# A fused decode step and its gradients: the first batch's w1 sums spread over more iterations, and a later start of the second pass

## The chip, the cores and the metric

The kernel runs on one core of one Trainium2 chip. The metric is the device time of one execution in microseconds. Beside the times there is one profiled execution, in which every instruction and every DMA packet was recorded; all readings of engines and queues below come from it.

## What is computed

The program is one decoder block for a single new token in each of two sequences (batches), forward and backward in one launch. Cut to what matters:

```python
x  = A_x                                     # 2 x 1 x 640, bf16
q  = layernorm(x) @ wq                       # 32 heads of 128
s  = q . K^T * 128**-0.5                     # K, V: 2 x 32 heads x 4096 keys x 128
p  = softmax(s)
h  = x + (p . V) @ wo                        # attention and residual
h2 = h + relu(layernorm(h) @ w1) @ w2        # MLP, 640 -> 1728 -> 640
out_0 = h2
# and the gradients of h2, seeded with grad_out, by x, K, V, wq, wo, w1, w2:
# gV[key, :] = p[key] * go          gK[key, :] = gs[key] * q
```

The caches and their gradients are by far the largest data: for each of the 64 pairs of batch and head a K tile and a V tile of 1 MB (4096 x 128 in bf16) are read, and a gK tile and a gV tile of the same size are written. Here go is the gradient that reaches a head's output, and gs = p * (dp - dot), with dp = V . go and dot the sum of p * dp.

## The kernel before, in words

**Two passes over the pairs.** The gradient go of a batch is known only when the attention of all its heads, the output projection, the MLP and their backward have been gone through. So the kernel works in two passes. The first pass (p1_iter, iterations i = 0 to 65) takes one pair an iteration in a software pipeline of three stages: in iteration i the scores of pair i are computed (K is transposed on PE in groups, line 423, copied out of PSUM, line 428, and multiplied with the query, line 436), the softmax numerators of pair i-1 are formed (the row maximum, line 559, is spread over the partitions by a matmul, line 503, and its minimum taken, line 505; the exponential, line 512, gives ep; two multiplies on VectorE, line 464, weight the K tile with it and give the pk tiles), and the products of pair i-2 are summed on PE (line 457 with V, line 486 with K). The second pass (p2_iter, steps j = 0 to 64) takes one pair a step: it transposes the V tile again, computes dp, and writes gV and gK as outer products on VectorE (line 809), some of whose gV columns ScalarE makes (line 870) in the steps that run alone, up to j = 32. The gK and gV tiles leave by the POOL queue (lines 850 and 871).

**The middle between them.** For each batch a generator, middle_gen, computes what lies between: the last attention outputs, the second layernorm, the MLP's hidden layer, its backward and the go of each head. It is background work: the main loop calls bg_step after each of the eight parts k = 0 to 7 of an iteration, and it advances as far as a credit allows. Its costly parts are sums on VectorE (ttr, line 644: a multiply of two tiles with a sum along the row): 15 of 128 x 576 with w1 for the gradient of the layernorm's output, and after them 32 of 128 x 640 with wo, one a head, in groups; after a group, a few small instructions mark its heads as done ("go"). Before each such sum the generator asks turn() for a slot; the main loop sets the number of slots, slot[0], anew in each part of an iteration, and slots not used are gone.

**Where the passes meet.** Batch 0's middle is queued at the end of iteration 33. Then come M0_ITERS iterations of the first pass alone, in which it runs. At iteration P2_AT = H + 2 + M0_ITERS = 41 the second pass begins: from there a step j runs beside every two iterations i, and after iteration 65 the remaining steps run alone. If the go of a step's head is not yet done when the step begins, bg_until forces the middle on. P2_AT also switches some helpers: before it the pk column that sums ep (line 474) and the copy of p (line 547) are made on POOL, from it on ScalarE (line 476) and VectorE.

**Buffers and queues.** K and V tiles come through the SP queue, in a list made beforehand, each into the next free of 12 buffers of 1 MB; a load waits, at the head of its queue, for the buffer's last reader. The V tiles of the last six heads of batch 0 (KEPT) stay in their buffers from the first pass to the second, which takes these six heads first; the other V tiles are loaded a second time (W tiles). At P2_AT and after, some buffers pass to the gK and gV tiles. The w1 matrix is loaded once, near iteration 35. A further set of generators, for the gradients of w1, w2, wo, wq and x, starts when batch 1's w1 sums are done, and stores by the ACT queue.

Of the kernel before, what the change touches and what calls it, by code (L numbers as in the profile page):

```python
# [15 lines left out]
def kernel(  # L16
# [582 lines left out]
    def a_heads(i):  # L599

        if a_next[0] < o_next[0]:
            a_group()
        elif o_next[0] < NP1 // OG and i >= o_next[0] * OG + OG + 2:
            b, g = divmod(o_next[0], H // OG)
            if b > 0 or i >= W_AT[g * OG * 4 // H] + 4:
                o_group()
# [40 lines left out]
    slot = [99]  # L647
# [399 lines left out]
    done = set()  # L1047
# [16 lines left out]
    def bg_step(k, rate):  # L1064
        step[0] += int(k == 1)
        q = (bg, bg2, bg3)[k]
        credit[k] = min(credit[k] + rate, 1.0 if k else 2.0) if q else 0.0
        while q and credit[k] > 0.0:
            took = bg_one(q)
            credit[k] -= took  # L1070
            if took == 0.0:
                break
# [5 lines left out]
            assert bg and bg_one(bg) >= 0.0, mark  # L1078
        forced[0] = False

    M0_ITERS = 7
    P2_AT = H + 2 + M0_ITERS
    RATES = (0.2, 0.8, 0.2, 0.8, 0.45)
    RATE2 = 0.65
# [28 lines left out]
    def pump():  # L1113
        while queue:
            what, k = queue[0]
            if what == "w":
                load_weights(k)
            else:
                tag = "ld"
                if free["ld"] < 1:  # L1120
                    return
                if what == "w2":
                    w2_tiles[k] = load_w2(k, tag)
                else:
                    load_tile(what, k, tag)
            queue.pop(0)
# [12 lines left out]
    def p2_step():  # L1139
        nonlocal g2  # L1140
        try:
            next(g2)
        except StopIteration:
            g2 = None

    for n, (i, j) in enumerate(plan):
# [42 lines left out]
        if i is None:  # L1189
            spread[0] = 2  # L1190
            at_k[0] = 1
            k = 0
# [10 lines left out]
        for k, _ in enumerate(p1_iter(i, i < H + 1, 0)):  # L1203
            for _ in range(at.get(k, 0)):
                if g2 is not None:
                    p2_step()
            if k == 5:
                a_heads(i)
            pump()

            spread[0] = 1 if i < P2_AT else 2
            at_k[0] = k
            if i >= P2_AT:
                slot[0] = int(k == 6 or (k == 1 and j is None))
            elif i > H + 1:
                slot[0] = {1: 2, 3: 1, 4: 1, 6: 1}.get(k, 0)
            else:
                slot[0] = int(k in (1, 6))
            bg_step(0, rate)
            bg_step(1, 0.0)  # L1220
# [43 lines left out]
```

## Time and profile before

| | |
|---|---|
| median of 3 runs | 896.87 us (896.23 to 898.17) |
| profiled execution, its own time | 895.05 us |
| its span, first to last instruction or transfer | 893.3 us |
| mean granted TensorE clock | 0.776 of full |
| PE, DVE, ACT, POOL busy | 83%, 77%, 54%, 23% of the span |
| moved by DMA | 362.89 MB, mean 406 GB/s |
| iterations 34 to 40, first pass alone with batch 0's middle | 211.67 to 256.96 us, by the row maxima |
| first gV store | 267.95 us |

How to read it: the page's slices cut the span into 40 equal parts; a digit is the busy share of an engine in tenths, and the GB/s row gives what the DMA queues moved. The windows view gives the same for stretches that one chooses. The timeline lists instructions with their start, their length and, in brackets, the time their engine stood idle before them and what ended that wait; starts of one instruction that comes once an iteration give the iteration's length. The busy share of PE is not a measure of how near it is to its limit, since the ends of its pipelined matmuls are modelled. The waits view sums, for each pair of instructions, how long one waited for the other. An iteration's row maximum is the instruction at line 559; the one of iteration 30, for example, started at 190.11 us.

### The profile page before, as it was taken

Reading aid. Unit: us, or ns where it says so; the run is one execution under the profiler, and the core shown is the slowest. Engines: PE = TensorE matmul, PEld = TensorE weight load, DVE = VectorE, ACT = ScalarE, POOL = GpSimd, SP = SyncE. Lnnn points to the kernel's source line nnn. Section 1 sums busy time; section 2 is a strip of 40 time slices with the busy share of each in tenths; the row PEclk is TensorE's granted clock in tenths of the full one; section 3 lists DMA queues with packets and bytes.
Section 4 is the critical chain, followed back from the end, with each engine's and each line's share of the span. In section 5 each row is a group of like instructions: output and inputs, shape, how many; then the busy total and the mean of one; then the engine's idle time right before and its main releaser. Section 6 shows DMA issues by size and latency. Waiting matters only on the chain.

```text
span 893.3 us, 24580 instructions
## 1 busy us (share of the span) xinstructions
PE 742.4 (83%) x10145; PEld 619.6 (69%) x10145; DVE 686.8 (77%) x1284; ACT 482.9 (54%) x1242; POOL 208.0 (23%) x349
## 2 busy tenths in 40 slices
PE   4999899999998997988968777877887889578780
PEld 4888788788887886877757766666765566366460
DVE  2566788777878897786878887878896469999872
ACT  1344334344555554554536767777675666367560
POOL 1344434443211111010011242222221111111120
PEclk9999999999999999998995556555565565565565
DMA  9999999999889999999999999999999999999996
GB/s 378 425 419 417 416 408 417 426 423 367 314 322 357 424 424 425 424 423 425 420 406 394 420 422 416 411 415 421 416 424 415 408 386 425 425 425 424 427 422 294
DMA packets 56432, 362.89 MB, mean 406 GB/s; under 512 B 5696, under 2 KB 11776, under 8 KB 15488
## 3 DMA queue, kind: packets, MB, share of 16 engines
q1 hardware_dynamic: 34664, 212.17, 58.2%
q0 software_dynamic: 18432, 134.23, 36.1%
q10 hardware_dynamic: 3224, 14.92, 4.1%
q8 instruction: 80, 1.31, 0.5%
q14 instruction: 32, 0.26, 0.1%
HBM read 212.16 MB, written 149.13 MB: 404 GB/s over the span
## 4 chain that ended last, share of the span: by engine, by line
PE 45%; DMA 26%; DVE 12%; ACT 9%; issue 4%; SPq 0%; POOL 0%; ACTq 0%; POOLq 0%; DVEq 0%
PE t_ps L423 19%; DMA Vt<-in_A_v_cache_dram 11%; PE m_ps L457 10%; DMA out_dram<-gV 7%; DMA out_dram<-gK 5%; PE s_ps L436 3%; ACT gV L870 3%; DVE gV L809 3%; PE u_ps L486 3%; ACT t_sb L428 3%; DMA wqs<-in_A_wq_dram 3%; PE o_ps L908 2%; PE dp_ps L436 2%; DVE gK L809 2%; DVE pk L464 2%
## 5 line engine op out<-in xcount | busy, mean ns | idle before, releaser
L428 ACT COPY t_sb<-t_ps 128x512 f32<-128x512 f32 x479 | 273.6, 586 | 188.9 <-PE t_ps L423 183.2
L436 PEld LDWEIGHTS <-t_sb 128*128 128x128 bf16 x4096 | 179.2, 102 | 58.8 <-ACT t_sb L428 32.7
L423 PE MATMUL t_ps<-ident_f,Wt 128*128 128x128 f32 x848 | 198.8, 384 | 0.2 <-ACT t_sb L428 0.2
L457 PE MATMUL m_ps<-pk,Vt 128*128 128x129 bf16 x2048 | 172.5, 223 | 12.9 <-DMA Vt<-in_A_v_cache_dram 11.4
L464 DVE TENSOR_TENSOR pk<-Kt,ep 128x2048 bf16<-128x2048 bf16 x128 | 156.4, 1223 | 30.1 <-ACT ep L512 14.2
L423 PE MATMUL t_ps<-ident_f,Kt 128*128 128x128 f32 x1024 | 158.6, 289 | 4.4 <-DMA Kt<-in_A_k_cache_dram 4.3
L809 DVE TENSOR_TENSOR gK<-rb,gsp 128x2048 bf16<-128x2048 bf16 x128 | 152.7, 1227 | 10.7 <-DMA out_dram<-gV 8.6
L423 PEld LDWEIGHTS t_ps<-ident_f,Wt 128*128 128x128 f32 x848 | 139.0, 200 | 25.2 <-issue 18.0
L457 PEld LDWEIGHTS <-Vt 128*128 128x128 bf16 x2048 | 125.9, 99 | 43.4 <-issue 29.7
L809 DVE TENSOR_TENSOR gV<-rb,pp 128x2048 bf16<-128x2048 bf16 (+1 forms) x128 | 142.6, 1139 | 8.1 <-DMA out_dram<-gK 7.8
L474 POOL COPY pk<-ep 128x16 bf16<-128x16 bf16 x80 | 84.3, 1056 | 161.2 <-ACT ep L512 86.8
L423 PEld LDWEIGHTS t_ps<-ident_f,Kt 128*128 128x128 f32 x1024 | 115.1, 147 | 8.3 <-issue 3.7
L436 PE MATMUL dp_ps<-gom,t_sb 128*128 128x2 bf16 x2048 | 95.9, 168 | 20.9 <-ACT t_sb L428 20.4
L871 POOL DMA_DIRECT2D out_dram<-gV x64 | 34.3, 536 | 288.0 <-DVE gV L809 157.4
L436 PE MATMUL s_ps<-qm,t_sb 128*128 128x2 bf16 x2048 | 87.7, 164 | 1.2 <-DVE t_sb L426 1.2
L850 POOL DMA_DIRECT2D out_dram<-gK x64 | 34.1, 533 | 219.8 <-DVE gK L809 162.6
L571 ACT CAST MT<-m_ps 128x128 bf16<-128x128 f32 x64 | 17.1, 267 | 106.7 <-PE m_ps L457 106.6
L914 ACT CAST ot<-o_ps 128x512 bf16<-128x512 f32 (+3 forms) x152 | 67.5, 491 | 4.2 <-DMA out_dram<-ot 2.4
L822 DVE SCALAR_TENSOR_TENSOR gsp<-dp_ps,negdot,P_bf 128x64 bf16<-128x64 f32 x64 | 17.9, 280 | 60.9 <-PE dp_ps L436 60.6
L836 ACT ACTIVATE rb<-dp_ps,rt 128x256 bf16<-128x256 f32 x64 | 30.1, 471 | 42.1 <-PE dp_ps L831 40.7
L644 DVE CUSTOM_DVE_ANT_0 junk<-wo_t,hbc 128x640 bf16<-128x640 bf16 x64 | 52.5, 821 | 0.5 <-ACT hbc L625 0.2
L644 DVE CUSTOM_DVE_ANT_0 gxj<-wqs,gqr 128x1024 bf16<-128x1024 bf16 x40 | 48.8, 1219 | 1.4 <-DMA wqs<-in_A_wq_dram 1.2
(200 smaller groups left out, 765.6 us busy)
## 6 DMA issues: line engine op xcount, KB each, us to landing
Kt<-in_A_k_cache_dram SPq DMA_DIRECT2D x64, 1024.0 KB, 15.0
Vt<-in_A_v_cache_dram SPq DMA_DIRECT2D x64, 1024.0 KB, 13.4
out_dram<-gV POOLq DMA_DIRECT2D x64, 1024.0 KB, 13.2
out_dram<-gK POOLq DMA_DIRECT2D x64, 1024.0 KB, 14.2
Wt<-in_A_v_cache_dram SPq DMA_DIRECT2D x53, 1024.0 KB, 12.9
wq_t<-in_A_wq_dram SPq DMA_DIRECT2D x5, 1024.0 KB, 6.8
wo_t<-in_A_wo_dram SPq DMA_DIRECT2D x4, 1280.0 KB
wqs<-in_A_wq_dram SPq DMA_DIRECT2D x5, 1024.0 KB, 16.8
```

What stands on the lines that cost most here:

```text
L423: nc.tensor.transpose(t_ps[:, j, :], natf[:, 2 * cc:2 * cc + 2, :].rearrange("p c k -> p (c k)"), ident_f[:])
L428: nc.scalar.copy(out=t_sb[:], in_=t_ps[:])
L436: nc.tensor.matmul(dst[:, sc:sc + 2], lhsT=v[:, j, :, par], rhs=vecs[:, par, :], start=(par == 0), stop=(par == 1))
L457: nc.tensor.matmul(r["m"][:, 0:129], lhsT=r["V"][:, sc, :], rhs=r["pk"][sc // HALF][:, sc % HALF, 0:129], start=(sc == 0), stop=(sc == NSC ...
L464: nc.vector.tensor_tensor(out=p["pk"][k][:, :, 0:128].rearrange("p s (a two) -> p s a two", two=2), in0=p["K"][:, sl, :].rearrange("p s (a ...
L474: nc.gpsimd.tensor_copy(out=col, in_=e)
L644: nc.vector.tensor_tensor_reduce(out=junk[0:kc, 0:width], in0=in0, in1=in1, scale=1.0, scalar=0.0, op0=ALU.mult, op1=ALU.add, accum_out=acc)
L809: nc.vector.tensor_tensor(out=pairs_view(dst[:, sl, :]), in0=row.rearrange("p (a two) -> p a two", two=2)[:, None, :, :].to_broadcast([128 ...
L836: nc.scalar.activation(out=rb[:], in_=bank[:, 128:384], func=ACT.Copy, scale=rt[:, b, h:h + 1])
L850: nc.gpsimd.dma_start(out=natural(out_2, bp, hp), in_=gK[:])
L871: nc.gpsimd.dma_start(out=natural(out_3, b, h), in_=gV[:])
L914: nc.scalar.copy(out=ot[0:P, k, n0:n0 + nn], in_=o_ps[0:P, 0:nn])
```

## The change

Two values change. M0_ITERS goes from 7 to 9, so that the second pass begins at iteration 43. And in the iterations between 33 and the start of the second pass, the slots depend on whether batch 0's w1 sums are done: until then there is one slot each in parts 1, 4 and 6 of an iteration, three in all; after that the five of before, two in part 1 and one each in parts 3, 4 and 6.

```diff
-    M0_ITERS = 7
+    M0_ITERS = 9
     P2_AT = H + 2 + M0_ITERS
...
             elif i > H + 1:
-                slot[0] = {1: 2, 3: 1, 4: 1, 6: 1}.get(k, 0)
+                slot[0] = ({1: 2, 3: 1, 4: 1, 6: 1} if ("w1", 0) in done else {1: 1, 4: 1, 6: 1}).get(k, 0)
```

The list of loads, plan and the helpers that turn at P2_AT follow from P2_AT. In the program that comes out, the w1 sums of batch 0 fall on iterations 36 to 41 in place of 36 to 39, the first pair of go marks on iteration 42 in place of 40, and the order of the background work from iteration 66 on is as before, each part of it beside a second-pass step whose number is lower by one. The second pass has 13 steps begun by iteration 65 in place of 14, and 52 steps alone where it had 51.

## The prediction

> **What bounds the kernel now.** I read the page first, for the time scale and the rates.
>
> ```profile
> span 893.3 us, 24580 instructions
> PEclk9999999999999999998995556555565565565565
> DMA  9999999999889999999999999999999999999996
> GB/s 378 425 419 417 416 408 417 426 423 367 314 322 357 424 424 425 424 423 425 420 406 394 420 422 416 411 415 421 416 424 415 408 386 425 425 425 424 427 422 294
> ```
>
> A slice is 22.3 us. The DMA row is full nearly everywhere and the rate stands near 425 GB/s: the program moves 362.89 MB, and most of its length is the time to move them. The last store is issued at 877.33 us (timeline) and the span runs on to 893.3, so the end too is transfers draining. Time can be won or lost almost only where the rate sags; the largest sag is slices 9 to 12, some 200 to 290 us, which is the stage this change edits. I cut it at the row maxima (rmax, one an iteration) and asked for the windows:
>
> ```profile
> 190.11:195.48 5.37, 5.37 (x92) 4.75 (x92) 3.69 (x8) 2.45 (x9) 2.87 (x5) 1.00 1.02 427
> ...
> 231.34:237.57 6.23, 5.94 (x98) 5.09 (x96) 6.16 (x16) 3.99 (x11) 1.22 (x4) 1.00 0.83 306
> 237.57:244.05 6.48, 5.75 (x91) 4.77 (x91) 6.38 (x17) 3.41 (x10) 1.37 (x3) 1.00 0.89 336
> 244.05:250.34 6.29, 5.51 (x107) 4.74 (x108) 6.08 (x20) 2.58 (x8) 1.24 (x3) 1.00 0.91 349
> 250.34:256.96 6.62, 6.48 (x105) 5.86 (x105) 5.28 (x17) 3.24 (x11) 1.16 (x4) 1.00 0.88 319
> ```
>
> Columns: length, busy time of PE, PE weight loads, DVE, ACT, POOL, granted clock, DMA share, GB/s. The first row is iteration 30, the others 37 to 40. In 37 and 38, with five w1 sums each, DVE is busy 99% of the time and DMA only 83 to 89%. An iteration brings one K and one V tile, 2 x 1024 KB = 2.097 MB, which is 4.93 us at 425 GB/s: all beyond that is lost DMA time. The same view later, where both passes run together and where the second runs alone:
>
> ```profile
> 302.57:318.76 16.19, 15.02 (x255) 12.77 (x253) 13.75 (x30) 9.51 (x27) 1.31 (x3) 1.00 1.01 425
> ...
> 457.14:490.00 32.86, 21.46 (x296) 19.25 (x297) 22.86 (x50) 15.65 (x41) 6.21 (x15) 0.64 1.00 402
> 490.00:700.00 210.00, 166.18 (x1598) 134.33 (x1597) 169.69 (x299) 148.22 (x376) 55.84 (x99) 0.56 1.01 418
> ```
>
> Both are full. Last, PE's timeline at the matmul that spreads the row maxima (line 503), one an iteration, and one later wait:
>
> ```profile
> 190.84 0.22 PE L503 MATMUL s_ps<-neg_ident,rmax 128*128 128x128 bf16 x1
> 196.06 0.22 PE L503 MATMUL s_ps<-neg_ident,rmax 128*128 128x128 bf16 x1
> 201.77 0.22 PE L503 MATMUL s_ps<-neg_ident,rmax 128*128 128x128 bf16 x1
> ...
> 231.68 0.22 PE L503 MATMUL s_ps<-neg_ident,rmax 128*128 128x128 bf16 x1
> 237.80 0.23 PE L503 MATMUL s_ps<-neg_ident,rmax 128*128 128x128 bf16 x1 [0.52 <-DVE rmax L559]
> 244.29 0.23 PE L503 MATMUL s_ps<-neg_ident,rmax 128*128 128x128 bf16 x1 [0.74 <-ACT t_sb L428]
> 250.48 0.22 PE L622 MATMUL bc_ps<-ident_bf,gh1c 128*128 128x128 bf16 x1 [0.67 <-DVE asum L596]
> 251.41 0.22 PE L503 MATMUL s_ps<-neg_ident,rmax 128*128 128x128 bf16 x1
> ```
>
> Undisturbed, PE alone sets the pace: 5.22 us from one spread to the next, 5.71 with an attention-output group. From 231.68 to 251.41 it is 6.12, 6.49 and 7.11, and PE, which works in order, stands at waits for DVE results (the ACT name at 244.29 is of a copy long done; rmax started at 244.05). PE's waits here are DVE's backlog.
>
> **The change, part by part.** Durations are of the profiled execution: span 893.3, time 895.05 us, 1.82 below the median 896.87 of the runs shown. I add the difference found to the median.
>
> ```profile
> L644 DVE CUSTOM_DVE_ANT_0 junk<-w_t,fbc 128x576 bf16<-128x576 bf16 x15 | 11.3, 755 | 0.5 <-ACT fbc L625 0.3
> SPq L444 <- DVE pk L464: 48.0, 8, 7.3
> ```
>
> (1) *Sums spread.* The 15 sums stay, 755 ns each plus an 81 ns accumulator read, 0.82 with what overlaps. They lie 3, 5, 5, 2 over iterations 36 to 39; afterwards 2, 3, 3, 3, 3, 1 over 36 to 41. DVE's demand in an iteration like 37 falls from 6.2 to 6.23 - 2 x 0.82 = 4.6 us, under PE's 5.22. The slots kept lie behind the row maximum, behind ep's activation and between the two pk multiplies, where the iteration without sums shows DVE idle or, between the multiplies, a 0.68 us copy. What PE loses now: 6.12 + 6.49 + 7.11 = 19.72, against 3 x 5.22 + 0.49 for the attention group + 0.20 for the column sum of the backward norm + 11 broadcast matmuls at 0.05 (four at 232.21 took 0.22) = 16.9: 2.8 us, of which 1.93 are the idle entries above. Iteration 36 gives nothing: PE had no idle time in it. Remaining afterwards I take 0.15 in each of four iterations with three sums and 0.4 in that with the backward norm, 1.0: **-1.8 us**. Bounds of the remainder: none (-2.8), or three fifths of today's 0.94 in each of four iterations plus a full 0.94, 3.2 (+0.4). I sit near the first, since DVE's demand comes out below PE's.
>
> (2) *Two more iterations of the first pass alone.* Pace 5.22 to 5.39 (mean of four: 5.22, 5.71, 5.41, 5.22); I take 5.28, so 10.56 us. Their two K and two V tiles are then no longer moved in the joint stage, which is full at 425 GB/s: 4.194 MB, 9.87 us back. Net **+0.7 us** (0.6 to 0.9). This holds while loads keep up: six of twelve tiles are parked V tiles of batch 0 in this stage, and the SP row shows what that does, the K and V loads waiting for the second pk multiply to free a tile. The V tile issued at 231.45 landed at 236.34, after 4.9 us, and its first matmul began at 237.90, 6.45 after the issue; at the faster pace that is about 5.6, so 0.7 are left. DMA is told by a page as well: the Trainium skill, "DMA: Bandwidth & Descriptors", "Where 436 GB/s comes from", gives a port ceiling of 435.2 GB/s. By that the four tiles give back 9.64 and the sum below would be -0.8; the rows' 425 decides.
>
> (3) *One step of the second pass moves.* 12 steps start beside the first pass by iteration 63 now, 11 afterwards; 52 run alone in place of 51. Each moves a W load and two stores, 3.146 MB: 7.40 us at the joint stage's 425 GB/s, 7.53 at the lone stage's 418: **+0.1 us**. The compute it brings (16 transposes, 32 matvecs, four DVE multiplies, eight ACT products of gV in place of DVE's, one POOL copy) hides under those transfers; without that cover a lone step costs its mean spacing, 8.17 us (gsp from 465.90 to 874.37, 50 steps): +0.8. On SP the first fetched W tile slips two iterations of K and V loads and one W load goes behind the last wq tile; POOL's stores start two iterations later and one pair of them more falls into the lone stage. With the queues full that is order, not bytes: 0, bounds -0.5 to +0.5 (the lost rate of one slice such as 386 against 408).
>
> (4) *Helpers that turn with the pass's start.* In iterations 41 and 42 four pk-column copies go to POOL in place of ACT (0.26 us there) and two P copies to POOL in place of DVE (0.17). POOL takes 0.25 to 1.33 us for the former, but in 211.67 to 256.96 the waits have it standing 19.4 us for ep, and no PE wait names it: 0. Without that cover, 4 x 1.07 = +4.3; below nothing, -0.35 on DVE. The rule that speaks against: the Trainium skill, "SBUF — State Buffer", "Who interferes with whom", has a DVE instruction with two SBUF inputs hold off GpSimd reads, which the pk multiplies and the sums would do. By it these copies run at the long end, and the sum would be +3.3 if PE came to wait for them.
>
> (5) *Background work.* All of batch 0's middle sits two iterations later. It has 30 more sums behind the first group, at one or two slots an iteration; it ends in iteration 65 in place of 63, still before batch 1's middle is queued. From iteration 66 on the order is the same with the second pass one step back: 0.
>
> Sum: -1.8 + 0.7 + 0.1 = **-1.0 us**: 892.3 span, 895.9 against the median.
>
> **The rivals.**
> (B) *More comes back.* The first joint pair, 256.96 to 271.00, moves 286 GB/s at a share of 0.79: 2.9 us idle, part of it the backlog carried in. If DVE enters it clean and half goes, with a remainder of none in (1): -2.0 - 1.45, 893.4. For it: DVE is not late by iteration 42 in the new spread. Against: that pair waits for ACT copies too, 0.47 at 260.50, and PE is busy 13.57 of its 14.04.
> (C) *Hidden anyway.* The DMA queue has other slack and the stage's gain is spent at the next wait for V: 896.9. Against: the queue is idle, not late, in this stage, so nothing absorbs a gain.
> (D) *Slower: the moved step.* The PE clock is 0.64 from 457 to 490 and 0.56 after it; four lone steps take 32.86 us there at 402 GB/s, and a step at 465.90 takes 10.57. If the first lone step, now one earlier, finds the tile pool as poor, it costs 10.6 and not 7.5: +3.1 - 1.0 = +2.1, 899.0. It cancels the gain from 8.5 us for the step and is slower by over 0.2% from 10.3.
>
> **How the numbers follow.** 0.2% is 1.8 us, about what a measurement of this kernel tells from no change; the three runs span 1.9. My case 0.45, its own range from the bounds of (1) to (3): 894.3 to 897.9; about 0.12 of it lies below 895.1. B 0.25, all faster. C 0.09, the same. D 0.21, of which 0.03 stays within the bound. So faster 0.37, same 0.45, slower 0.18. The range takes B's 893.4 and D's 899.0 as ends, with 0.3 for the spread of the runs: 893.1 to 899.3.
>
> **What would show it.** Right: in iterations 37 to 40 spreads 5.2 to 5.7 us apart, no wait for rmax over 0.2, DVE busy about 5 of 5.5 us, DMA share 0.9 or more there; two more iterations before the first gV store; the store's start some 8 to 9 us later than 267.95; 425 GB/s unchanged from 300 to 440. Wrong: spreads still near 6 with PE waiting for pk or for POOL; a V wait in the stage; or a lone step of over 10 us more around 450 to 490, with the rate under 400 there.

## The result, and the profile after

The change made the kernel slower: 903.26 us (median of 22 runs, 897.79 to 909.55) against 897.78 us for the kernel before (22 runs beside them, 895.3 to 903.13). The ratio is 1.0053, 95% interval 1.0036 to 1.007. Taken once more in a later comparison (12 runs, `after_3` below) it was 1.0027, 1.0005 to 1.005. The change therefore costs some 0.3 to 0.5%, 2.4 to 4.8 us. The forecast was a gain of 1.0 us, and 903.26 lies above its range. Both kernels scatter by several us from one execution to the next, so one profile against another says little; where it matters, several are set side by side.

The profiled execution of the kernel after took 903.91 us. These are its span, clock and DMA rows, in the 40 slices of the page:

```profile
span 901.7 us, 24613 instructions
...
PEclk9999999899999898998985555555565555565555
DMA  9999999999898999999999999999999999999997
GB/s 378 423 419 416 416 407 418 425 415 353 315 357 318 378 392 379 423 427 423 422 408 383 421 420 419 420 420 419 420 420 410 374 399 425 426 424 424 425 424 314
```

The sag that began at slice 9 ended with slice 12 before. Now it reaches slice 15 (379 GB/s), which is deep in the stage that runs both passes. Slices 31 and 32 (374 and 399) are the second place that got worse.

The stage that the change edits, in windows cut at the row maxima of iterations 37 to 42 (columns as in the prediction: length, busy PE, PE weight loads, DVE, ACT, POOL, clock, DMA share, GB/s):

```profile
234.32:239.22 4.90, 4.90 (x91) 4.28 (x90) 4.84 (x11) 2.55 (x6) 2.54 (x3) 1.00 0.80 279
239.22:245.01 5.79, 5.77 (x96) 4.97 (x94) 5.11 (x13) 3.60 (x11) 2.90 (x5) 1.00 1.00 406
245.01:250.86 5.85, 5.85 (x112) 5.09 (x111) 5.08 (x13) 3.06 (x9) 2.75 (x4) 1.00 0.98 385
250.86:256.58 5.72, 5.72 (x96) 5.10 (x95) 4.95 (x11) 3.03 (x10) 1.66 (x3) 1.00 0.99 391
256.58:262.01 5.43, 5.43 (x97) 4.96 (x96) 5.26 (x18) 2.71 (x7) 0.61 (x3) 1.00 0.85 287
262.01:269.66 7.65, 6.28 (x102) 5.47 (x100) 6.12 (x22) 3.83 (x13) 2.20 (x4) 1.00 0.94 368
```

And PE's timeline at the spreading matmul, with the one wait over 0.4 us:

```profile
234.74 0.22 PE L503 MATMUL s_ps<-neg_ident,rmax 128*128 128x128 bf16 x1
240.15 0.22 PE L503 MATMUL s_ps<-neg_ident,rmax 128*128 128x128 bf16 x1
245.58 0.22 PE L503 MATMUL s_ps<-neg_ident,rmax 128*128 128x128 bf16 x1
251.59 0.22 PE L503 MATMUL s_ps<-neg_ident,rmax 128*128 128x128 bf16 x1
257.00 0.22 PE L503 MATMUL s_ps<-neg_ident,rmax 128*128 128x128 bf16 x1
262.59 0.22 PE L503 MATMUL s_ps<-neg_ident,rmax 128*128 128x128 bf16 x1
264.17 0.64 PE L457 MATMUL m_ps<-pk,Vt 128*128 128x129 bf16 x8 [1.37 <-DMA Vt<-in_A_v_cache_dram]
269.90 0.23 PE L503 MATMUL s_ps<-neg_ident,rmax 128*128 128x128 bf16 x1
```

The waits for rmax and asum are gone, and PE is busy all but 0.02 us of iterations 38 to 41: that part of the forecast came true. But PE now stands 1.37 us at a V tile in iteration 42, and even where PE runs without a gap the DMA rate is 385 to 406 and not 425. The stall on DVE has been exchanged for one on the loads. The three further profiles with the same code up to there (`after_2`, `after_3` and `after_share`, all described below) have a wait for V at the same place, of 1.09, 1.10 and 1.75 us.

**Where the time is.** Both kernels move the same 362.89 MB, so a kernel is later by the transfer time that it loses. For a stretch that is its length times (1 - rate/425). The two kernels, in the windows from the spread of iteration 37 to the first joint pair, over the first twelve iterations of the joint stage (six pairs of one second-pass step each), and over iterations 94 to 97; first before, then after:

```profile
231.68:257.20 25.52, 23.59 (x399) 20.23 (x396) 23.80 (x65) 13.28 (x37) 4.85 (x13) 1.00 0.88 331
257.20:350.05 92.85, 85.78 (x1448) 74.84 (x1447) 78.54 (x162) 54.38 (x151) 11.96 (x17) 1.00 0.97 392
...
678.65:725.49 46.84, 39.58 (x328) 28.43 (x327) 19.73 (x21) 29.09 (x59) 5.25 (x12) 0.50 0.99 396
```

```profile
234.74:269.90 35.16, 33.66 (x577) 29.46 (x574) 31.17 (x82) 18.84 (x53) 12.66 (x19) 1.00 0.94 359
269.90:369.44 99.54, 91.06 (x1446) 80.29 (x1447) 77.41 (x156) 54.51 (x151) 11.94 (x17) 0.91 0.95 371
...
681.02:727.86 46.84, 39.60 (x328) 28.43 (x327) 19.73 (x22) 29.10 (x59) 5.22 (x12) 0.50 0.96 381
```

The loss is 5.6, 7.2 and 3.2 us before, and 5.5, 12.6 and 4.9 after. The same, from the unrounded bytes, for every profile that bears on it ("37 to start" ends at the spread of the iteration in which the second pass starts, "pairs" are the first six steps beside the first pass; `before_share_late` is the kernel before up to iteration 88, `after_share` the kernel after up to there):

| profile | 34-37 | 37 to start | pairs | to 66 | 66-94 | 94-98 | 98 to end |
|---|---|---|---|---|---|---|---|
| before | 2.7 | 5.7 | 7.3 | 1.4 | 4.7 | 3.2 | 6.9 |
| before_2 | 2.7 | 5.6 | 8.8 | 4.3 | 6.0 | 3.8 | 5.6 |
| before_share_late | 4.3 | 5.7 | 9.6 | 1.7 | 5.4 | 5.6 | 5.5 |
| after | 4.4 | 5.6 | 12.7 | 1.2 | 4.5 | 4.8 | 5.9 |
| after_2 | 3.7 | 6.2 | 7.1 | 2.5 | 6.7 | 6.2 | 5.9 |
| after_3 | 3.8 | 5.6 | 7.5 | 1.6 | 5.7 | 5.8 | 5.7 |
| after_share | 2.2 | 7.4 | 12.1 | 2.3 | 6.1 | 4.1 | 6.0 |
| kept_5_before | 2.0 | 5.2 | 8.0 | 3.0 | 4.8 | 3.6 | 7.2 |
| kept_5_after | 5.2 | 4.9 | 8.1 | 2.2 | 5.4 | 2.7 | 8.2 |
| after_5_share | 2.0 | 4.4 | 7.6 | 5.6 | 7.9 | 0.1 | 7.9 |
| kept_4_before | 2.7 | 5.5 | 7.8 | 2.2 | 5.8 | 4.0 | 5.2 |
| kept_4_after | 0.6 | 3.2 | 7.3 | 2.4 | 6.9 | 2.3 | 6.9 |
| after_4_share | 1.5 | 4.3 | 7.4 | 1.6 | 7.2 | 0.0 | 8.6 |

Means of the kernel after (four profiles, three from 94 on) less means of the kernel before (three, two from 94 on): 37 to start +0.5, where the forecast said -1.1; pairs +1.3, with a scatter as large; 94 to the end +1.7; the rest about +0.1. The sum, 3.6, lies between the two measured differences of the medians, 3.1 us (901.37 against 898.3) and 5.5.

### The profile page after: what moved, and what is told of

Read it like the earlier page. It is cut to its first block, busy times and chain, and to the rows that moved or that the text cites. A ratio compares the mean times of both kernels' runs of the same rounds, so it can differ in the third digit from the quotient of the medians.

```text
span 901.7 us, 24613 instructions
## 1 busy us (share of the span) xinstructions
PE 752.5 (83%) x10145; PEld 629.9 (70%) x10145; DVE 686.5 (76%) x1282; ACT 484.8 (54%) x1246; POOL 211.7 (23%) x356
## 2 busy tenths in 40 slices
DMA packets 56432, 362.89 MB, mean 402 GB/s; under 512 B 5696, under 2 KB 11776, under 8 KB 15488
## 4 chain that ended last, share of the span: by engine, by line
PE 46%; DMA 24%; DVE 13%; ACT 9%; issue 5%; SPq 1%; POOL 0%; ACTq 0%; POOLq 0%; DVEq 0%
PE t_ps L423 19%; DMA Vt<-in_A_v_cache_dram 12%; PE m_ps L457 10%; DMA out_dram<-gK 7%; DVE gV L809 4%; ACT gV L870 3%; PE s_ps L436 3%; DMA out_dram<-gV 3%; DVE gK L809 3%; PE u_ps L486 3%; PE o_ps L908 2%; PE dp_ps L436 2%; ACT t_sb L428 2%; DMA Kt<-in_A_k_cache_dram 2%; DVE junk L644 2%
## 5 line engine op out<-in xcount | busy, mean ns | idle before, releaser
L423 PE MATMUL t_ps<-ident_f,Wt 128*128 128x128 f32 x848 | 207.0, 397 | 0.4 <-ACT t_sb L428 0.4
L423 PEld LDWEIGHTS t_ps<-ident_f,Wt 128*128 128x128 f32 x848 | 144.6, 206 | 28.9 <-issue 22.8
L474 POOL COPY pk<-ep 128x16 bf16<-128x16 bf16 x84 | 91.4, 1090 | 168.4 <-ACT ep L512 85.8
L870 ACT ACTIVATE gV<-rb,pa 128x128 bf16<-128x128 bf16 x160 | 48.9, 392 | 0.0
## 6 DMA issues: line engine op xcount, KB each, us to landing
Vt<-in_A_v_cache_dram SPq DMA_DIRECT2D x64, 1024.0 KB, 12.6
Wt<-in_A_v_cache_dram SPq DMA_DIRECT2D x53, 1024.0 KB, 10.8
wo_t<-in_A_wo_dram SPq DMA_DIRECT2D x4, 1280.0 KB, 20.5
```

The source lines that it names most:

```text
L423: nc.tensor.transpose(t_ps[:, j, :], natf[:, 2 * cc:2 * cc + 2, :].rearrange("p c k -> p (c k)"), ident_f[:])
L474: nc.gpsimd.tensor_copy(out=col, in_=e)
L870: nc.scalar.activation(out=gV[:, NSC - act + k, :], in_=c["rb"][:, 0:128], func=ACT.Copy, scale=pa[:, k:k + 1])
```

## The experiments

| kernel | runs | median us | ratio to before (95%) |
|---|---|---|---|
| late_only | 7 | 909.92 | 1.0119 (1.009 to 1.0148) |
| sums_doubled | 8 | 905.94 | 1.0078 (1.0045 to 1.011) |
| start_45 | 12 | 904.81 | 1.0064 (1.0039 to 1.0089) |
| four_at_41 | 12 | 902.22 | 1.0031 (1.0011 to 1.005) |
| four_at_42 | 12 | 900.26 | 1.002 (0.9996 to 1.0044) |
| after_vfirst | 6 | 905.29 | 1.0083 (1.0053 to 1.0114) |
| kept_5_before | 12 | 897.54 | 0.9991 (0.9967 to 1.0015) |
| kept_5_after | 12 | 900.86 | 1.0015 (0.9991 to 1.0038) |
| kept_4_before | 12 | 898.48 | 0.9999 (0.9979 to 1.0019) |
| kept_4_after | 12 | 897.45 | 0.9997 (0.9979 to 1.0015) |
| after_3 | 12 | 901.37 | 1.0027 (1.0005 to 1.005) |
| after_share | 12 | 901.89 | 1.0024 (0.9998 to 1.0049) |
| before_share_late | 12 | 899.38 | 0.9992 (0.9965 to 1.0018) |
| after_5_share | 12 | 900.58 | 1.0013 (0.9984 to 1.0042) |
| after_4_share | 12 | 896.29 | 0.9966 (0.9943 to 0.9989) |

Each ratio is to runs of the kernel before on the same chip, whose median stood between 897.4 and 899.4 us.

### One part alone: the later start without the spread

```diff
-    M0_ITERS = 7
+    M0_ITERS = 9
```

> The second pass begins two iterations later, but the w1 sums stay at five an iteration. Before loses 39.3 us of its span to transfer rates under 425 GB/s, after 47.7; of the 8.4 between them 5.4 lie in the joint stage's first six pairs. Theory of the pace (three sums let the first pass run at 5.4 us an iteration, faster than the six free tiles are refilled, so that the joint stage begins without lead): here iterations 37 and 38 stay over 6 us, no wait for V before the joint stage, its first six pairs lose about 7 us as before, and the time is 0 to +0.2% of before. Theory of the start (beginning two iterations later costs the 5 us by itself, by the phase of the pairs or by one more lone step): +0.4 to +0.7%, the joint pairs losing 11 to 13 us.

> The later start alone once more, for a second profile: its first profile was of an execution of 901.7 us where the median was 909.9, so what the usual execution loses was not seen. Theory of the ring: at a time of 906 or more, the loss beyond the first profile (45.6 us in all, 7.7 in the first six joint pairs) lies in waits for V and K in the joint stage, 5 us or more there. Rival, chance outside: it lies before iteration 34 or in the lone steps.

The slowest kernel of all: 1.0119, beyond what either theory expected, and 908.62 us in one more execution (`late_again`). It loses 10.9 and 12.2 us between iteration 37 and the start (the first in a profile of its fastest execution, 901.66 us), twice what either kernel of the pair does. Its first six joint pairs lose 7.7 and 8.9 us (worked out as in the table), so the joint stage is not where its time goes, and the theory of the ring that was put on record for `late_again` did not hold. PE's timeline in its iterations 41 and 42 shows why:

```profile
255.87 0.23 PE L503 MATMUL s_ps<-neg_ident,rmax 128*128 128x128 bf16 x1
261.23 0.19 PE L339 MATMUL pr_ps<-goc,sel 128*128 128x4 bf16 x2 [1.28 <-DVE goc L667]
263.08 0.36 PE L674 MATMUL d_ps<-pr,ones_f32c 128*128 128x4 f32 x2 [1.23 <-DVE gom L344]
264.48 0.31 PE L503 MATMUL s_ps<-neg_ident,rmax 128*128 128x128 bf16 x1
271.05 0.23 PE L503 MATMUL s_ps<-neg_ident,rmax 128*128 128x128 bf16 x1
```

The w1 sums are done in iteration 39 there, and the slots left go to the sums with wo, four between one row maximum and the next from 255.63 to 270.81 us; PE waits 1.28 and 1.23 us for their marks, and the next two spreads come 8.61 and 6.57 us apart. So the two parts of the change pull in opposite directions: the later start alone costs 1.2%, and the spread takes 0.7 to 0.9 points of that back (1.0119 against 1.0053 and 1.0027). What has to be explained is why the later start, even with its slots filled well, still costs more than the spread is worth.

### The spread alone, or nearly

Four slots an iteration, with the old start and with one iteration more; the rest of the kernel after is kept.

```diff
-    M0_ITERS = 9
+    M0_ITERS = 7
...
-                slot[0] = ({1: 2, 3: 1, 4: 1, 6: 1} if ("w1", 0) in done else {1: 1, 4: 1, 6: 1}).get(k, 0)
+                slot[0] = ({1: 2, 3: 1, 4: 1, 6: 1} if ("w1", 0) in done else {1: 1, 3: 1, 4: 1, 6: 1}).get(k, 0)
```

> The spread without the later start: four w1 sums an iteration in place of five, second pass at iteration 41 as before; the first go marks are then half an iteration late and are forced at its beginning. Theory of the ring: VectorE's backlog shrinks and nothing is parked longer, so 0 to -0.2% of before. Rival (the spread itself does harm, through a first pass too fast for its loads): +0.2 to +0.5%, with a wait for V before iteration 43.

> Four w1 sums an iteration and the second pass at iteration 42, one later than before. Theory of the ring: half of the change's cost, +0.1 to +0.4%. Rival by phase (an odd start suits the order of K and V loads, an even one does not): +0.6% or more, over the change itself. Rival by pace: 0, since four sums keep VectorE busy to 5.4 us an iteration.

With the start at 41 the first pair's go marks are not ready and are forced. This is PE's timeline there, cut to the waits over 0.4 us and the spreads:

```profile
255.56 0.20 PE L339 MATMUL pr_ps<-goc,sel 128*128 128x2 bf16 x2 [1.83 <-DVE goc L667]
256.43 0.56 PE L674 MATMUL d_ps<-pr,ones_f32c 128*128 128x2 f32 x2 [0.67 <-DVE gom L344]
258.64 0.31 PE L503 MATMUL s_ps<-neg_ident,rmax 128*128 128x128 bf16 x1
268.26 0.22 PE L503 MATMUL s_ps<-neg_ident,rmax 128*128 128x128 bf16 x1
```

The iteration to 258.64 takes 9.82 us (its predecessor's spread stood at 248.82), and the first joint pair loses 8.0 us where before it lost 4.5. The ratio is 1.0031, where the theory of the ring expected 0 to -0.2%. A spread without a later start is paid for in this way; that is why the two come together. With the start at 42 the ratio is 1.002, between the two and told from neither.

### Later still

```diff
-    M0_ITERS = 9
+    M0_ITERS = 11
```

> The changed kernel with the second pass beginning at iteration 45, four later than before, so that the pairs of the joint stage have the phase against the groups of four heads that they had at 41. Theory of the pace: the first pass alone runs still longer at 5.4 us, so the joint stage begins without lead all the same: +0.4 to +0.8%. Theory of the start by phase: the first six pairs lose about 7 us as before, and the time is +0.1 to +0.2%. Theory of the start by lone steps: +1.0%, twice the change.

1.0064, not told apart from the change's own 1.0053, and a wait for V of 2.80 us at 263.92. Its profile, which is of the slowest of its 12 executions, loses 13.2 us between iteration 37 and the start at 45. Running the first pass alone still longer gains nothing: no sum is spread any further by this.

### Was the pace too fast? The sums made twice

In the kernel after, ten of the 15 w1 sums are made a second time, which puts five an iteration on DVE again while the start stays at 43.

```diff
             for c in range(ND):
                 yield from turn()
+                if b == 0 and at_k[0] in (1, 4):
+                    ttr(w1_t[:, c, k * FW:(k + 1) * FW], fbc[:, k * FW:(k + 1) * FW], gx2p[:, c, k:k + 1], FW)
                 ttr(w1_t[:, c, k * FW:(k + 1) * FW], fbc[:, k * FW:(k + 1) * FW], gx2p[:, c, k:k + 1], FW)
```

> The changed kernel with ten of the fifteen w1 sums made twice (the same values written again), so that VectorE has five sums in iterations 37 to 40 as the kernel before had in two. Theory of the pace: the iterations go back to 6.1 to 6.5 us, there is no wait for V in iteration 42, the joint stage's first six pairs lose about 7 us in place of 12.7, and the time is 0.2 to 0.4% over before, under the changed kernel. Theory of the start: the extra VectorE time comes on top, +0.7 to +1.0%.

PE's timeline has its waits for DVE back:

```profile
236.82 0.23 PE L503 MATMUL s_ps<-neg_ident,rmax 128*128 128x128 bf16 x1 [0.56 <-DVE rmax L559]
243.34 0.23 PE L503 MATMUL s_ps<-neg_ident,rmax 128*128 128x128 bf16 x1 [1.09 <-DVE rmax L559]
...
255.89 0.23 PE L503 MATMUL s_ps<-neg_ident,rmax 128*128 128x128 bf16 x1 [0.66 <-DVE rmax L559]
```

The wait for V before the start is gone with them, the stretch from 37 to the start loses 8.6 us, and the ratio is 1.0078. The first six pairs lose 11.7 us, where the theory of the pace expected about 7. The theory that the spread harms by running the first pass too fast for its loads is therefore wrong as a theory of the total: slowing that stage makes it worse. The spread is good; the loads behind it take part of its gain.

### The order of the loads

From iteration 43 on, the V tile of a pair is put ahead of the K tile in the list of loads.

```diff
+        if ii is not None and ii >= P2_AT:
+            queue.append(("V", ii - 2))
...
-        if ii is not None and ii >= 2:
+        if ii is not None and 2 <= ii < P2_AT:
```

> The changed kernel with one order turned: from iteration 43 on the V tile of an iteration stands before its K tile in the list of loads, so that each V tile takes the buffer that falls free one place earlier. Theory of the late V tile (the joint stage loses its 5 us over before in waits of 2 us and more for V, each followed by 3 to 10 us of half PE clock): the waits for V at the second and third pair go or fall under 1 us, the first six pairs lose 7 to 9 us in place of 12.7, and the time is 0 to +0.3% of before. Rival, the tiles are late whatever their order (too few buffers): waits for K take the place of those for V, +0.4 to +0.7%.

1.0083, more than either theory expected. From 228 to 450 us PE has one wait for V left, of 0.4 us, but seven for K tiles, 13.2 us in all; in the kernel after it waits 9.5 us for V and 2.9 for K there. The first six pairs lose 8.4 us in this profile, as the theory of the late V tile expected, and the time is no better for it. Which tile goes first only chooses who waits. That both are late because buffers are short is what the next experiment tests.

### The parked buffers: six, five or four kept tiles

`kept_5_*` and `kept_4_*` keep the V tiles of five or four heads of batch 0 in place of six, in the kernel before and in the kernel after. Each tile fewer is one buffer more for the first pass, and 1.05 MB more to move, 2.5 us at 425 GB/s.

```diff
-    KEPT = (6, 5)
+    KEPT = (4, 5)
```

> The kernel before with five parked V tiles in place of six: seven tiles for loads, one more V tile loaded a second time (2.5 us of transfers). With the changed kernel the same edit took the ratio from 1.0053 to 1.0015. Theory of the ring (a later start keeps the six tiles parked for two iterations more, and loads through six free tiles come too late): before is hardly starved, so it gains little and pays the load, +0.1 to +0.4%, and the changed kernel with five parked is no slower than this one. Rival, the fifth tile is simply better for either kernel: -0.1 to -0.4%, and the change costs 0.3 to 0.5% between these two as it does with six.

> The changed kernel with five parked V tiles of batch 0 in place of six: seven tiles are left for loads in the first pass's end, and one more V tile of 1 MB is loaded a second time, 2.5 us of transfers. Theory of the pace: the wait for V in iteration 42 (1.4 us) is gone, the first pairs lose 7 to 8 us in place of 12.7, and the time is 0 to +0.3% of before in spite of the extra load. Theory of the start: the extra load comes on top, +0.7 to +0.9%.

> The kernel before with four kept in place of six: the partner of kept_4_after. Both theories: 0.997 to 1.003 of the kernel before; only its distance to kept_4_after tells them apart.

> The kernel after with four V tiles of batch 0 kept in place of six; two more V tiles are loaded a second time (2.1 MB, 4.9 us at 425 GB/s) and two more buffers turn over in the first pass. Theory (the later start costs time mainly because six of twelve buffers stay parked two iterations longer, so that K and V loads go out one by one): no wait for V above 0.5 us in iterations 41 and 42, the six joint pairs lose 7 to 9 us and not 10 to 13, and the change is worth no more here than with five: ratio of the change, against kept_4_before, 1.000 to 1.002. Rival (the parked tiles do not matter, kept_5_after was a lucky draw): the change costs 0.5% here too.

> The kernel after once more, in the same call as the two with four kept tiles, so that the distances are taken on one chip: 1.0053 again, 1.0036 to 1.007.

What the change costs falls with the number of parked tiles: with six 0.53% and 0.27% (two comparisons), with five 0.24% (1.0015 less 0.9991, measured on two chips), with four -0.02% (0.9997 less 0.9999). Neighbouring steps are not told apart by their intervals; six and four are by the first comparison (0.36 to 0.70%). On one chip, `kept_4_after` against `after_3` is 897.45 against 901.37 us, while `kept_4_before` against the kernel before is 898.48 against 898.3. So two parked tiles fewer bring the kernel before nothing net of their 4.9 us of transfers, and the kernel after 3.9 us.

The trace shows the cause at the loads. These lines are from the view of the V tiles, with the count and the first and last issue from iteration 37 to the start of the second pass and the time from issue to landing. The kernel before, the kernel after, the kernel after with four kept tiles:

```profile
L444 SPq DMA_DIRECT2D Vt<-in_A_v_cache_dram x4: 327/328/328, 231.4 to 250.4; - x4
DMA to landing us min/median/max: 4.8/4.8/4.9
```

```profile
L444 SPq DMA_DIRECT2D Vt<-in_A_v_cache_dram x5: 327/328/328, 234.4 to 256.7; - x5
DMA to landing us min/median/max: 4.8/6.2/7.4
```

```profile
L444 SPq DMA_DIRECT2D Vt<-in_A_v_cache_dram x6: 328/328/328, 230.3 to 258.0; - x6
DMA to landing us min/median/max: 6.2/7.7/7.7
```

In the kernel after, the V tile of pair 40 is issued at 256.69, 0.03 us behind the end of the second pk multiply, with which a K tile's buffer comes free, and lands at 264.13. Its first matmul would have begun 6.1 us after the issue (264.17 - 1.37 - 256.69) and begins after 7.5. With four kept tiles the same tile is issued at 245.98, 12.5 us before the spread of the iteration that uses it (258.49). It may then take 7.7 us to land, and nobody waits. The timeline of that kernel has no wait for a V tile up to the start, only one for the row maximum; its last three spreads:

```profile
252.91 0.22 PE L503 MATMUL s_ps<-neg_ident,rmax 128*128 128x128 bf16 x1
258.49 0.22 PE L503 MATMUL s_ps<-neg_ident,rmax 128*128 128x128 bf16 x1
265.16 0.23 PE L503 MATMUL s_ps<-neg_ident,rmax 128*128 128x128 bf16 x1 [0.63 <-DVE rmax L559]
```

And the windows from iteration 37 to the start, first `kept_4_before`, then `kept_4_after`:

```profile
234.42:259.88 25.46, 23.59 (x400) 20.23 (x397) 23.74 (x65) 13.27 (x37) 4.71 (x13) 1.00 0.87 333
```

```profile
230.66:265.16 34.50, 33.72 (x577) 29.52 (x575) 31.09 (x82) 19.33 (x54) 11.57 (x19) 1.00 0.99 386
```

The loss falls from 5.5 to 3.2 us there, a gain of 2.3, where with six kept tiles it went from 5.7 to between 5.6 and 7.4. So the gain that the prediction forecast for this stage exists, and it is the parked buffers that took it. With four kept tiles nothing is left of the other two differences either: the pairs lose 7.3 us against 7.8, and the stretch from iteration 94 to the end 9.2 against 9.2 (one profile each).

They can take more in the joint stage. In the first profile (`after`) the kernel after waits for V in its third and fifth joint pairs, and near the end of each wait a spell begins in which the granted clock is half (6.8 us from 301.5, 10.2 us from 335.7); the eight matmuls that took 0.64 us at 264.17 take 1.05:

```profile
302.38 1.05 PE L457 MATMUL m_ps<-pk,Vt 128*128 128x129 bf16 x8 [2.54 <-DMA Vt<-in_A_v_cache_dram]
...
336.58 1.05 PE L457 MATMUL m_ps<-pk,Vt 128*128 128x129 bf16 x8 [1.79 <-DMA Vt<-in_A_v_cache_dram]
```

```profile
299.62:319.21 19.59, 16.68 (x250) 15.07 (x251) 13.07 (x24) 8.85 (x26) 2.23 (x3) 0.83 0.98 384
...
334.56:355.01 20.45, 18.29 (x260) 16.24 (x261) 13.14 (x27) 8.48 (x25) 2.24 (x3) 0.75 0.97 375
```

A pair at the full clock takes 15.4 us there, one with such a spell 19.6 or 20.5. All seven profiles with six kept tiles have a wait for V of 1.2 to 2.5 us between 287 and 303 us, in the third pair, those of the kernel before too. The ones with five or four kept tiles have none until 334 us, and lose 7.3 to 8.1 us in the six pairs, against 7.1 to 12.7.

### The step number in the shares of the buffers

From step j = 36 on (line 1163) some buffers pass between the loads, the stores' tiles and the last gradients. The background work goes by iteration, the steps now come one iteration later, and so this change of shares falls one step later against that work.

```diff
-        elif fin is not None and j >= H + KEPT[1] - 1:
+        elif fin is not None and j >= H + KEPT[1] - 2:
```

This is `after_share`, and with `KEPT = (5, 5)` or `(4, 5)` beside it `after_5_share` and `after_4_share`. `before_share_late` is the kernel before with `j >= H + KEPT[1]`.

> The kernel after with the threshold of one share of buffers moved one step back (j >= H + KEPT[1] - 2), so that the change of shares falls on the same iteration and the same point of the background work as in the kernel before. Theory (tiles are handed over by step number while the background work goes by iteration, and this is where iterations 94 to 98 lose 4.8 and 6.2 us of transfer time in two profiles of the kernel after, against 3.2 and 3.8 in two of the kernel before): the loss there goes back to 3.2 to 3.8, and the ratio to the kernel before from 1.0053 to 1.003. Rival (the loss there comes from the one W load more that is still to be made, which this edit leaves as it is): 4.6 to 6.2 again, ratio 1.005.

> The kernel before with the same threshold moved one step forward (j >= H + KEPT[1]): the change of shares falls on the point of the background work at which the kernel after has it, and nothing else moves. Theory: iterations 94 to 98 lose 4.6 to 6.2 us of transfer time in place of 3.2 to 3.8, and the time is 0.1 to 0.3% above the kernel before. Rival (the one W load more is the cause): 3.2 to 3.8, ratio 1.000.

> The kernel after with five V tiles kept in place of six and the threshold moved one step back. Five kept tiles alone gave a ratio of 1.0015, with a loss of 2.7 us in iterations 94 to 98, below the others. Theory of shares: nothing more to win at 94 to 98, 1.000 to 1.002. Rival (2.7 was chance and the shares do matter): 0.999 to 1.001.

> The kernel after with four kept tiles and the threshold of the share of buffers one step earlier. Four kept tiles brought the change back to the time of the kernel before (0.9997); with five kept tiles this threshold took the loss of iterations 94 to 98 to 0.15 us. Theory (both lie at buffers, and what they save adds up): a loss there under 1 us in place of 2.26, ratio 0.996 to 0.999. Rival (what is saved there is lost elsewhere, as the kernel before_share_late, with 5.57 us lost there, took no longer): the loss there may fall, the ratio stays at 0.999 to 1.001.

The windows of iterations 94 to 97, of `after_share`, `before_share_late` and `after_4_share` in this order:

```profile
679.78:726.62 46.84, 39.60 (x328) 28.43 (x327) 19.74 (x21) 29.12 (x59) 5.24 (x12) 0.50 0.97 388
```

```profile
687.60:734.44 46.84, 39.59 (x328) 28.42 (x327) 19.74 (x22) 29.12 (x59) 5.25 (x12) 0.50 0.97 375
```

```profile
673.51:716.82 43.31, 33.91 (x294) 25.37 (x294) 21.01 (x32) 27.30 (x56) 6.50 (x14) 0.55 1.01 425
```

The kernels before and after and these first two all need 46.84 us for these iterations, whatever the rate: compute sets the length there, and DMA carries more or less in it. A later share brings the rate of the kernel before down (396 and 390 to 375), an earlier one brings that of the kernel after up (381, 369 and 373 to 388), and with four kept tiles it is full. But part is given back after iteration 98. From 94 to the end the losses are: before 10.1 and 9.4, with the later share 11.0; after 10.7, 12.1 and 11.5, with the earlier share 10.1; five kept tiles 10.8, with it 8.1; four 9.2, with it 8.6. All four pairs go the same way, by 0.6 to 2.8 us; but each edit has one profile, profiles of one kernel differ by up to 1.4 us there, and `after_5_share` loses more than the others before it reaches iteration 94. One comparison also speaks against the shift as the whole cause: with five and with four kept tiles the change moves the share by the same step, and yet the kernels before and after lose the same from 94 to the end, 10.8 and 10.8, 9.2 and 9.2. The times do not confirm it one by one: `before_share_late` is not slower (0.9992, where 1.001 to 1.003 was expected), `after_share` (1.0024) lies below both measurements of the kernel after but inside the interval of the second, and `after_5_share` (1.0013) is told apart neither from `kept_5_after` (1.0015) nor from the kernel before. So the place is shown in the traces, and that the step of the share acts on it; that this is the whole of the 1.7 us, and its price in the time, is not.

`after_4_share` is the one version that beats both kernels: 896.29 against 899.39 us, 0.9966 with an interval below one, although it moves 364.99 MB in place of 362.89. It is the best of 14 variants and was measured in one comparison, so its 0.3% is more likely too large than too small.

### Repeats

> The kernel before once more, for a second profile. Theory of the late V tile: the first six pairs lose 7 to 8 us again, and no wait for V over 1.5 us before the fourth pair. Rival, chance: an execution of 901 us or more, with the joint pairs losing what the changed kernel lost.

> The changed kernel once more, for a second profile. Theory of the late V tile: again waits for V of 2 us or more in the first three pairs, and 3 us or more lost in the first six pairs over before's 7.3. Rival, chance: those pairs lose 7 to 8.5, and what the execution loses lies elsewhere.

899.15 and 901.10 us; their losses are in the table. The theory of the late V tile did not hold: the six pairs of `before_2` lose 8.8 us, where 7 to 8 were expected, and those of `after_2` no 3 us more but 7.1, with no wait for V over 1.2 us in its first three, where 2 us or more were expected. They showed that the 12.7 us of the first profile's joint pairs is not the rule (7.1 here, 7.5 in `after_3`, 12.1 in `after_share`), and that the 4.8 us at 94 to 98 is (6.2, 5.8).

## Why the prediction was wrong, by its own steps

**(1) Sums spread, -1.8.** The mechanism was right. From the spread of iteration 37 to that of 40 it took 16.85 us in place of 19.72 (some of the work in these, the backward norm above all, has moved to iteration 41); DVE is busy 4.95 to 5.11 us of 5.72 to 5.85, as forecast; no wait for rmax over 0.2 us. Undoing it at the same start (`late_only`, `sums_doubled`) costs 0.3 to 0.9 points. From 37 to the start the kernel before took 25.52 us; with two iterations of 5.28 that would be 36.08, and the kernel after took 35.16. The gain that was left is 0.9, not 1.8; the V wait of 1.37 us is more than the difference. The first gV store came at 281.0 us, 13.0 later than before, where 8 to 9 were forecast; 3.1 of this lie before iteration 37.

**(2) Two more iterations, +0.7, "this holds while loads keep up".** This is the first step that failed, by its clause "so 0.7 are left". The use was sized fairly (6.1 us after the issue, where 5.6 was forecast); the landing was not (7.4, where 4.9 was taken). The 4.9 was read in iterations in which DMA was idle 9 to 17% of the time. When the iteration shrinks to 5.4 us the K tile before it is still under way (issued at 239.65, landed at 247.88; the V tile was issued at 244.85), and the landing grows, 4.8, 6.2 and 7.4 us for the V tiles used in iterations 38, 40 and 42. The removal of one stall took away the slack that had made the next transfer look quick. The prediction had named a V wait in the stage as a sign of being wrong. Rival C said that "the stage's gain is spent at the next wait for V", and this happened; it was given 0.09 on the ground that an idle queue has nothing to absorb a gain. The kept tiles show that it could: a queue can be idle because no buffer is free. With two more buffers the DMA share of the stretch goes from 0.94 to 0.99.

**(2) again, the joint stage.** The working gave back 9.87 us of transfers "in the joint stage, which is full at 425 GB/s". Its first six pairs were not full before (7.3 to 9.6 us lost), and this holds no better after (7.1 to 12.7). The row that was shown for "full", 302.57 to 318.76, was the fourth pair.

**(3) One step moves, +0.1, and rival D.** Nothing shows here: the losses up to the first lone step are 1.2 to 2.5 us after and 1.4 to 4.3 before. D, the rival for slower, named one more lone step at 450 to 490 us that finds the pool poor and takes 10.6 us; this did not happen: one step there takes 10.5 us in `after`, as one of 10.57 did before. The sign was D's, the place was not: D had the sign by luck.

**(4) Helpers, 0.** Right: from iteration 37 to the start no PE wait of 0.4 us or more names POOL or those copies.

**(5) Background work, 0: "From iteration 66 on the order is the same with the second pass one step back: 0".** The second step that failed: from 94 to the end the kernel after loses 1.7 us more. Why is shown in part only. The order of each is the same, but one against the other they are shifted, and buffers change hands by the step number; moving the threshold back by a step brings the loss to 10.1 us in one profile, against 10.7 to 12.1 after and 9.4 and 10.1 before. But with five or four kept tiles the same shift costs nothing there, so the step number alone does not explain it.

The range ended at 899.3, because its upper end was taken from one mechanism in one place. What came were three smaller ones (0.5, 1.3 and 1.7 us in the means above, the second within the scatter of the profiles), of which the prediction had priced two at nothing. That the first was forecast as a gain of 1.1 makes the miss there 1.6 us. About 0.9 us of the miss is the base: the median before was 897.78 in the 22 runs, 896.87 in the three shown.

**What stays open.** The first six joint pairs of the kernel after lose 7 us in two profiles and 12 in two; which it will be is not decided by anything found here. From iteration 34 to 37, where both kernels execute the same instructions until part 3 of iteration 36, there is in some profiles a spell of 3.4 us at half clock that costs 1 to 2 us:

```profile
227.59 0.31 PE L503 MATMUL s_ps<-neg_ident,rmax 128*128 128x128 bf16 x1
```

This is from the timeline of `kept_4_before`, where the matmul takes 0.31 us in place of 0.22. The spell is in `before_share_late` too, and in `after`, `after_2`, `after_3`, `kept_5_after` and `after_4_share`, but not in `before`, `before_2`, `after_share` or `kept_4_after`: the change does not bring it about, though whether it makes it more frequent can't be said.

## What to carry to other kernels

A landing time read in a stretch where the queues are partly idle may be the shortest that a load has (4.8 us here, against 6.2 to 7.7 with more under way); ask what it becomes when the stretch gets faster, and whether the next load can be issued any earlier, or stands at a buffer that something parked holds. When two streams of work are shifted against each other, look for everything that is keyed to the counter of one and serves the other (buffer shares, thresholds), even if the order within each stays the same. And where a kernel scatters by 1% between executions, one profile can show a mechanism but not its share: here the largest loss of the first profile came in only two of four.

## What was not expected of the hardware

Where loads are issued one by one, they do not reach 425 GB/s even while the DMA share is near one: 406, 385 and 391 GB/s at shares of 1.00, 0.98 and 0.99 in the windows of iterations 38 to 40. In the packet records of the kernel after, packets of 8 KB take 309 ns as a rule; the first sixteen after a pause of 1.7 us, at 235.4 us, took 580 to 1330 ns.

Spells of half clock of 3.4, 6.8 and 10.2 us (multiples of 3.4) were seen about waits of PE for a V tile: 6.8 us with a wait of 2.5 and 10.2 with 1.8 in the kernel after, 3.4 with 1.2 in `after_2` and `after_3`; but none with 1.2 us in the kernel before, nor with the 1.37 us at 264.17 in the kernel after. The pair with the wait of 1.79 us took 5.1 us longer than its neighbour of 15.35. The spell of 3.4 us from 226.4 in the kernel after has none: from 180 to 232 us the waits view of PE is empty. That a wait sets a spell off, and what decides whether it does, is not shown.
